# Sign bits of decoded weights on GpSimd, squares on ScalarE, and more operands inside the plan

## The chip, the cores and the metric

One core of one Trainium2 chip runs the whole kernel. The metric is the device time of one execution in microseconds (us). TensorE (PE) has its weight loads beside it (PEld); VectorE is DVE, ScalarE is ACT, GpSimd is POOL, and SyncE (SP) issues most transfers. Line numbers "L450" are those of the kernel before; after the change a line's number is higher, by one up to L449, by seven from L459 on (L601 becomes L608), by up to nine near the end.

## The reference

```python
def _attn_ref(q, k, v, sampled_blocks):          # q, k, v: (4, 8, 768, 64)
    scores = scale * np.matmul(q, k.transpose(0, 1, 3, 2))
    ...   # block 32: neighbours, first and last block, and 3 sampled blocks per block row are kept
    attn = np.exp(scores - max); attn = attn / (sum(attn) + 1e-09)
    return np.matmul(attn, v)
def _moe_ref(x, w_in, w_out, s, b):              # x (3072, 512), w_in (512, 2048), w_out (2048, 512)
    h = x @ w_in
    r = np.maximum(h, 0.0)
    g = s * (r * r) + b
    return (g @ w_out)
```

The attention's output, laid out again as 3072 tokens of 512 numbers, is x. The weights w_in and w_out come as 64-bit floats.

## The kernel before

**Three stages.** From 0 to some 246 us the kernel does the block-sparse attention. From there to 378.6 us it does the first 32 blocks of the MLP, "the planned MLP stage". A block i is 128 hidden rows f by 384 tokens g. It has twelve matmuls mlp1(i) (384 columns) into the bank h; then relu (L443, ACT), square, hidden_high (L454: times s and plus b on ACT; L455: rounded to the high part gh on ACT), hidden_low (L459: the rest, the low part, on DVE); and nine matmuls mlp2(i) (512 columns, L480 to L482) that need gh and the low part, one block later. From 378.6 us to the end the rest of the tokens is done in products of half blocks, written out by hand: for each of eight passes p and each s from 1 to 3 seven products n in the order 1, 2, 6, 7, 5, 3, 4 (a Strassen-like scheme). Twelve matmuls of L617 make two products. Their operands are sums S1 to S4 of quarters of the weights and T1 to T4 of quarters of x, and the quarters A11 to A22, B11 to B22. An operand is split into a high part (cast on ACT, L599) and a low part (subtraction on DVE, L601). The first product of a pass is copied out of its bank by ACT (L1456); n = 2, 5, 3 and 4 are "taken" by DVE (L627 and L628, or L1465 for a sum ahead of it), and the output blocks (L480 to L482) stand between products.

**Names of operand steps.** "<T1" loads a quarter, "+S1" or "+T1" adds (L575, L577, L580), "wA21" puts a quarter of the weights together from its two parts (L584), "hS1" is the high part, "lS1" the low part, ">A21" writes a quarter back. Which steps are done in the planned stage and which at a product is written out in tables: `early` items in the plan, EARLY (behind the last two blocks, 30 and 31, which are written out), FIRST (at the products of the first pass), and F_NEXT (later passes).

**Weights.** Each of 32 tiles of 128 × 512 weights (16 of w_in, 16 of w_out) is decoded by `decode_f64` from its 64-bit words: two masks on DVE (L85, L87), a copy of 16-bit halves on GpSimd (L88), a sign on ACT (L89: Sign of the upper word in place, after both masks), two activations on ACT (L91, L92) that make the magnitude, the product of magnitude and sign on DVE (L93, the high part), its exponent (L94), and the low part (L95). Three raw tiles are used in turn. Six weights are decoded during attention, 26 beside the planned MLP blocks.

**The order of the work.** A list scheduler (`Plan`) orders the first two stages, up to block 29: every operation has a given engine, a cost in ns and a priority, and each engine's program is written in the order in which the scheduler would start them. Engines take their programs in order, so one that waits holds up what is behind it. Attention's softmax works in groups: four masked maxima (L966), the copy of a transposed tile (L1017), a reciprocal (L989, L990), and the scaled block xss (L1064), which TensorE transposes (L1070).

Of the kernel before, what the change touches and what calls it, by code (L numbers as in the profile page):

```python
# [9 lines left out]
F32 = mybir.dt.float32  # L10
# [3 lines left out]
U16 = mybir.dt.uint16  # L14
AF = mybir.ActivationFunctionType
ALU = mybir.AluOpType
# [23 lines left out]
def decode_f64(nc, n, src, top, most, raw_of, mag_of, low_of, hi_of, lo_of):  # L40
# [32 lines left out]
    def hi():  # L73
        return get("hi", hi_of)
# [4 lines left out]
    def low_half(k):  # L79
        return low(U16).rearrange("p (n two) -> p n two", two=2)[:, :, k]  # L80

    A, V, G = nc.scalar, nc.vector, nc.gpsimd
# [6 lines left out]
        ("a", lambda: A.activation(word(1).bitcast(F32), word(1).bitcast(F32), AF.Sign), (0, 1)),  # L89
# [3 lines left out]
        ("v", lambda: V.tensor_tensor(out=hi(), in0=mag(F32), in1=word(1).bitcast(F32), op=ALU.mult), (3, 5)),  # L93
# [119 lines left out]
def kernel(  # L213
# [238 lines left out]
    def hidden_high(i):  # L452
        t, gh = htile(i % 2), htile(2 + i % 3)
        nc.scalar.activation(t, t, AF.Identity, bias=sb_b, scale=sb_s if i >= T["SQ"] else 1.0)  # L454
        nc.scalar.copy(gh, t)  # L455

    def hidden_low(i, eng=None):
        t, gh = htile(i % 2), htile(2 + i % 3)
        (eng or nc.vector).tensor_tensor(out=htile(5 + i % 3), in0=t, in1=gh.bitcast(F32), op=ALU.subtract)  # L459
# [201 lines left out]
    with ExitStack() as es:  # L661
# [665 lines left out]
        cost = (400, 420, 800, 670, 720, 720, 550, 390, 690)  # L1327
# [13 lines left out]
        for k, (which, f) in enumerate((w[0], int(w[1:])) for w in T["WL"].split()):  # L1341
# [5 lines left out]
            for m in range(pieces):  # L1347
                last_load = op("s", 450, wat - 4 + 4 * m, lambda load=load, m=m, n=pieces: load(m, n), [prev_k], alloc=[] if m else [raw], use=[raw] if m else [],
                                order=[last_load, *[y for x, y in pv_at if x <= wat - 4 + 4 * m][-1:]] if k < EARLY_W else [last_load, xl[(0, 1)]], nbytes=524e3 / pieces, late=T["LATE"])
                loads.append(last_load)  # L1350
# [29 lines left out]
        for k in range(NPL):  # L1380
            g, f = subs[k]
            for c in range(NCC):
                pm = op("p", 490, N + T["M1"] + k, lambda k=k, c=c: mlp1(k, (c,)), cols=1152, deps=[*ends, xs_ops[(g, c, 1)], wdone[("i", f, 8)], hd.get((k - 2, 0))], order=[pm])
            dep = pm
            for m, (eng, c, fn) in enumerate((("a", 480, relu), ("a" if k >= T["SQ"] else "v", 510, square), ("a", 960, hidden_high), ("g" if k < T["LOW"] else "v", 1100 if k < T["LOW"] else 420, hidden_low if k >= T["LOW"] else lambda i: hidden_low(i, nc.gpsimd)))):
                dep = hd[(k, m)] = op(eng, c, N - 50 + k, lambda k=k, fn=fn: fn(k), [dep, o_t, hd.get((k - 2, 3)) if m == 0 else None,
                                      m2.get(k - 3) if m == 2 else None])
            if k > 0:
                g, f = subs[k - 1]
                pm2 = m2[k - 1] = op("p", 1930, N + T["M2"] + k, lambda k=k: mlp2(k - 1), cols=4608, deps=[*every, hd[(k - 1, 3)], wdone[("o", f, 8)]], order=[pm2])  # L1390
# [4 lines left out]
        def early(deps, what):  # L1395
            rest = what[1:] not in ("B11", "B21")
            eng = {"h": "a", "<": "s", ">": "s"}.get(what[0], "v")
            wide = what[1] in "BT"
            cost = {"a": 980 if wide else 350, "s": 450, "v": 950 if wide else 420}[eng]

            def fn():
                ready_first()
                if rest:
                    ready_rest()
                work(0, S0, what)

            ew[what] = op(eng, cost, N + 600 + len(ew), fn, [*(over if rest else [m2[14], m2[15], last_load]), *(ew[x] for x in deps.split())],
                          nbytes={"<": 393e3, ">": 131e3}.get(what[0], 0))
# [19 lines left out]
    FIRST = {2: "lT1 lS1 wA12 +S4 hS4 hB22", 6: "lS4 +T4 hT4", 7: "lB22", 5: "lT4"}  # L1428
# [5 lines left out]
    EARLY = {30: "hT3 lT3 hS3 lS3", 31: "<B22 hT2 lT2 hT1 hS1"}  # L1434
# [128 lines left out]
```

## Time and profile before

| | |
|---|---|
| median of three runs (770.6, 777.41, 770.78) | 770.78 us |
| profiled execution | 773.25 us, of which the span is 771.5 |
| busy | PE 730.2, PEld 618.8, DVE 561.4, ACT 473.2, POOL 241.1 us |
| attention, to about | 246 us |
| planned MLP stage, to about | 378.6 us |

The span lies 1.75 us inside the profiled execution's time. The windows below give an engine's busy time in a stretch; a row of the timeline names in brackets how long the engine sat idle ahead of it, and for whom. Several instructions of the same kind in a row are one line, with their count.

### The profile page before, as it was taken

The page shows a single profiled execution, that of the slowest core. Times are in us where ns is not written, and L with a number is a line of the kernel's source. Part 1 is how long each engine was busy: PE and PEld are TensorE (multiplying, and loading weights), DVE is VectorE, ACT ScalarE, POOL GpSimd, SP SyncE. Part 2 cuts the span into 40 slices and gives each one's busy share as a digit, 9 for nine tenths or more (in the row PEclk, how much of TensorE's full clock was granted, in tenths as well). Part 3 has the DMA queues.
Part 4 walks back from the last instruction along what each step waited for, and adds up shares of the span by engine and source line. Part 5 has one row for each costly group of instructions (what it writes and reads, how often), then busy time and mean ns, then how long its engine had stood idle before and what let it go on. Part 6 is the DMA issues. An engine that isn't in the chain of part 4 may idle for free.

```text
span 771.5 us, 21375 instructions
## 1 busy us (share of the span) xinstructions
PE 730.2 (95%) x8032; PEld 618.8 (80%) x8032; DVE 561.4 (73%) x1433; ACT 473.2 (61%) x1141; POOL 241.1 (31%) x398
## 2 busy tenths in 40 slices
PE   8799798799888999999989999999999999999997
PEld 6376675477566989999878998888998998888896
DVE  4667576688786789887896678687678679666652
ACT  3657576688776877789753444565444467444443
POOL 4846255345430121222022232223222232222221
PEclk9989999999999999999999999999999999999999
DMA  9987988857873534635433222224000022000002
GB/s 243 221 214 206 249 218 234 215 159 211 226 199 106 151 110 147 209 119 161 99 125 91 76 84 74 62 69 123 1 1 1 1 62 82 1 1 0 1 1 82
DMA packets 101110, 89.41 MB, mean 116 GB/s; under 512 B 50192, under 2 KB 79504, under 8 KB 101008
## 3 DMA queue, kind: packets, MB, share of 16 engines
q1 hardware_dynamic: 98704, 81.76, 37.7%
q0 software_dynamic: 2304, 6.29, 3.3%
q8 instruction: 63, 1.03, 0.6%
q14 instruction: 39, 0.32, 0.1%
HBM read 69.15 MB, written 14.68 MB: 109 GB/s over the span
## 4 chain that ended last, share of the span: by engine, by line
PE 76%; DVE 7%; ACT 5%; DMA 5%; issue 4%; POOL 1%; SPq 1%; POOLq 0%; ACTq 0%; DVEq 0%
PE m L617 20%; PE o L481 10%; PE o L482 10%; PE o L480 10%; PE s L949 5%; PE xs L1058 5%; PE t L1006 5%; PE h L438 2%; PE h L440 2%; PE h L439 2%; PE od L1048 2%; DMA xd<-xst 2%; PE xs L1070 1%; DMA qr_3s<-in_q_dup_dram 1%; DVE ptile L966 1%
## 5 line engine op out<-in xcount | busy, mean ns | idle before, releaser
L459 POOL TENSOR_TENSOR hid<-hid,hid 128x384 fp32r<-128x384 f32 x96 | 105.3, 1098 | 292.9 <-ACT hid L635 249.4
L634 ACT ACTIVATE hid<-hid,sb_b,sb_s 128x384 f32<-128x384 f32 x96 | 68.1, 710 | 152.2 <-DVE hid L628 152.2
L978 ACT ACTIVATE ptile<-ptile,nm 128x256 f32<-128x256 f32 (+1 forms) x208 | 107.3, 519 | 35.7 <-DVE nm L966 35.3
L966 DVE CUSTOM_DVE_ANT_1 ptile<-s,mt 128x256 f32<-128x256 f32 x176 | 64.4, 421 | 31.9 <-PE s L949 29.6
L482 PE MATMUL o<-woutr,hid 128*128 128x512 f32 x168 | 66.4, 395 | 0.0
L481 PE MATMUL o<-woutr,hid 128*128 128x512 f32 x168 | 66.3, 395 | 0.0
L480 PE MATMUL o<-woutr,hid 128*128 128x512 f32 x168 | 65.3, 389 | 0.0
L617 PE MATMUL m<-wout,win 128*128 128x384 f32 x264 | 62.6, 340 | 2.1 <-ACT xrest L1456 1.6
L1058 PEld LDWEIGHTS xs<-vA,pt 128*32 128x32 f32 x1696 | 36.0, 113 | 29.0 <-ACT xst L1075 8.2
L617 PE MATMUL m<-xp,wop 128*128 128x384 f32 x288 | 58.3, 337 | 0.0
L1006 PE MATMUL t<-ident,ptile 128*128 128x128 f32 x352 | 51.4, 289 | 6.7 <-ACT ptile L978 3.8
L628 DVE SCALAR_TENSOR_TENSOR hid<-hid 128x384 f32<-128x384 f32 x96 | 54.7, 569 | 3.3
L1058 PE MATMUL xs<-vA,pt 128*32 128x64 f32 x1696 | 48.0, 227 | 9.5 <-issue 4.3
L481 PE MATMUL o<-win,hid 128*128 128x512 f32 x144 | 56.8, 395 | 0.0
L617 PE MATMUL m<-xp,win 128*128 128x384 f32 x288 | 55.1, 338 | 1.4 <-DVE xp L601 0.7
L617 PEld LDWEIGHTS m<-xp,win 128*128 128x128 f32 x288 | 50.9, 188 | 4.6 <-DVE xp L601 1.2
L635 ACT CAST hid<-hid 128x384 fp32r<-128x384 f32 x96 | 49.4, 515 | 7.8 <-ACT hid L634 0.7
L617 PEld LDWEIGHTS m<-xp,wop 128*128 128x128 f32 x288 | 51.5, 188 | 2.1
L617 PEld LDWEIGHTS m<-wout,win 128*128 128x128 f32 x264 | 47.4, 188 | 5.1 <-ACT xrest L1456 2.5
L1006 PEld LDWEIGHTS t<-ident,ptile 128*128 128x128 f32 x352 | 39.1, 145 | 14.4 <-ACT ptile L978 5.7
L888 POOL COPY kk<-kt 128x256 f32<-128x256 f32 (+2 forms) x46 | 20.9, 457 | 93.8 <-PE s L949 93.7
L482 PE MATMUL o<-win,hid 128*128 128x512 f32 x126 | 49.8, 395 | 0.0
(187 smaller groups left out, 1859.0 us busy)
## 6 DMA issues: line engine op xcount, KB each, us to landing
vB<-in_v_dram SPq DMA_DIRECT2D x109, 128.0 KB, 3.7
vA<-in_v_dram SPq DMA_DIRECT2D x72, 128.0 KB, 3.9
raw_o<-in_w_out_dram SPq DMA_DIRECT2D x14, 512.0 KB, 3.3
raw_i<-in_w_in_dram SPq DMA_DIRECT2D x12, 512.0 KB, 3.8
xd<-xst SPq DMA_DIRECT2D x44, 128.0 KB, 3.5
out_dram<-ob SPq DMA_DIRECT2D x20, 256.0 KB, 2.0
sum<-xd SPq DMA_DIRECT2D x12, 384.0 KB, 4.2
kt<-in_k_blk_dram SPq DMA_DIRECT2D x8, 384.0 KB, 5.4
```

What stands on the lines that cost most here:

```text
L459: (eng or nc.vector).tensor_tensor(out=htile(5 + i % 3), in0=t, in1=gh.bitcast(F32), op=ALU.subtract)
L480: nc.tensor.matmul(acc, gh[:, tsl], wout(f, 0), start=first, stop=False)
L481: nc.tensor.matmul(acc, gh[:, tsl], wout(f, 1), start=False, stop=False)
L482: nc.tensor.matmul(acc, gl[:, tsl], wout(f, 0), start=False, stop=last)
L617: nc.tensor.matmul(to, w_, x_, start=(c == 0 and k == 0), stop=(c == 1 and k == 2))
L628: vec.scalar_tensor_tensor(out=t, in0=t, scalar=0.0, in1=t, op0=ALU.max, op1=ALU.mult)
L634: nc.scalar.activation(t, t, AF.Identity, bias=sb_b, scale=sb_s)
L635: nc.scalar.copy(gh, t)
L966: nc.vector.tensor_tensor_reduce(out=pt, in0=sp, in1=msk, scale=-scale, scalar=FMAX if g == 0 else nm[:, 0:1], op0=ALU.add, op1=ALU.min, a ...
L978: nc.scalar.activation(pt[:, :w], pt[:, :w], AF.Exp, bias=nms[n][:, last:last + 1], scale=-1.0, accum_out=dns[i][:, g, j:j + 1])
L1006: nc.tensor.transpose(tp[:, (2 * j + c) * P:(2 * j + c + 1) * P], src[:, c * P:(c + 1) * P], ident)
L1058: nc.tensor.matmul(xs[quads[pair]], pt[:, c, quads[pair]], vt[:, a, col:col + D], start=(j == 0 and c == 0), stop=(c == 1), tile_position= ...
```

## The change

(a) The sign leaves ACT: GpSimd compares the upper 16 bits with 2^15 and multiplies by −2, which leaves 0 or −2 as a 16-bit number in the raw tile; this step waits for the load alone. L93 becomes (sign + 1) × magnitude in one DVE instruction (SCALAR_TENSOR_TENSOR). (b) The squares of blocks 10 to 23 go from DVE (L450) to ACT (L448). (c) For blocks 0 to 9, whose square holds the factor s already, hidden_high is one activation into the high part instead of two steps, and hidden_low adds b and subtracts on DVE in one instruction. (d) The plan's costs are new, and the extra delay that it gives to raw loads goes from 3000 to 700 ns for the weights beside the MLP. (e) T4, hT2, lT2, hS3, lS3, hS1, lS1, S4, hS4, lS4 and others are steps of the plan and no longer of FIRST and EARLY; B11 and B21 wait for mlp2(18) and not for the last raw load.

```diff
-        ("a", lambda: A.activation(word(1).bitcast(F32), word(1).bitcast(F32), AF.Sign), (0, 1)),
+        ("g", lambda: G.tensor_scalar(out=half(0).bitcast(I16), in0=half(3), scalar1=2.0 ** 15, scalar2=-2.0, op0=ALU.is_ge, op1=ALU.mult), ()),
...
-        ("v", lambda: V.tensor_tensor(out=hi(), in0=mag(F32), in1=word(1).bitcast(F32), op=ALU.mult), (3, 5)),
+        ("v", lambda: V.scalar_tensor_tensor(out=hi(), in0=half(0).bitcast(I16), scalar=1.0, in1=mag(F32), op0=ALU.add, op1=ALU.mult), (3, 5)),
...
-    "WARM": 4, "FILL": 4, "FP": -1.0, "NPL": 30, "SQ": 24, "LATE": 3000.0, "M1": 75.6, "M2": 77.7,
+    "WARM": 4, "FILL": 4, "FP": -1.0, "NPL": 30, "SQ": 10, "LATE": 3000.0, "M1": 75.6, "M2": 77.7,
...
     def hidden_high(i):
-        nc.scalar.activation(t, t, AF.Identity, bias=sb_b, scale=sb_s if i >= T["SQ"] else 1.0)
-        nc.scalar.copy(gh, t)
+        if i < T["SQ"]:
+            nc.scalar.activation(gh, t, AF.Identity, bias=sb_b)
+        else:
+            nc.scalar.activation(t, t, AF.Identity, bias=sb_b, scale=sb_s)
+            nc.scalar.copy(gh, t)
...
     def hidden_low(i, eng=None):
+        if i < T["SQ"]:
+            nc.vector.scalar_tensor_tensor(out=htile(5 + i % 3), in0=t, scalar=sb_b, in1=gh.bitcast(F32), op0=ALU.add, op1=ALU.subtract)
+            return
...
-        cost = (400, 420, 800, 670, 720, 720, 550, 390, 690)
+        cost = (420, 460, 900, 900, 720, 720, 690, 460, 740)
...
-                                order=[...], nbytes=524e3 / pieces, late=T["LATE"])
+                                order=[...], nbytes=524e3 / pieces, late=T["LATE"] if k < EARLY_W else 700.0)
...
-        for deps, what in (("", "<B11"), ("", "<B21"), ("", "<T1"), ("", "<T3"), ("", "<T2"), ("", "<T4"), ("<B11", "hB11"), ("hB11", "lB11"),
-                           ("<B21", "hB21"), ("hB21", "lB21"), ("", "wA21"), ("", "wA22"), ("wA21 wA22", "+S1"), ("", "wA11"), ("+S1 wA11", "+S2"),
-                           ("+S2", "hS2"), ("<T3 <T1", "+T3"), ("+T3 <T2", "+T1"), ("+T1", "+T2"), ("hS2", "lS2"),
-                           ("+S2", "+S3"), ("+S3", ">A21")):
+        for deps, what in (("", "<B11"), ("", "<B21"), ("<B11", "hB11"), ("hB11", "lB11"), ("<B21", "hB21"), ("hB21", "lB21"),
+                           ("", "<T1"), ("", "<T3"), ("", "<T2"), ("", "<T4"), ("", "wA21"), ("", "wA22"), ("wA21 wA22", "+S1"), ("", "wA11"),
+                           ("+S1 wA11", "+S2"), ("+S2", "hS2"), ("hS2", "lS2"), ("+S2", "+S3"), ("+S3", ">A21"), ("<T3 <T1", "+T3"),
+                           ("+T3 <T2", "+T1"), ("+T1", "+T2"), ("+T2", "hT2"), ("hT2", "lT2"), ("+S3", "hS3"), ("hS3", "lS3"), ("+S1", "hS1"),
+                           ("hS1", "lS1"), ("", "wA12"), ("wA12 +S2", "+S4"), ("+S4", "hS4"), ("hS4", "lS4"), ("+T2 <T4", "+T4")):
...
-    FIRST = {2: "lT1 lS1 wA12 +S4 hS4 hB22", 6: "lS4 +T4 hT4", 7: "lB22", 5: "lT4"}
+    FIRST = {2: "hB22", 6: "hT4", 7: "lB22", 5: "lT4"}
...
-    EARLY = {30: "hT3 lT3 hS3 lS3", 31: "<B22 hT2 lT2 hT1 hS1"}
+    EARLY = {30: "hT3 lT3 hT1", 31: "<B22 lT1"}
```

TensorE's program is in the same order before and after; those of ACT, DVE, POOL and SP are not. Three places follow.

ACT at the end of the planned stage, before. L599 with 128x256 is the high part of a sum of weights (hS2 goes into "win", hS3 into "wop"), with 128x12x2x32 that of a quarter of x or a sum T; L443, L448, L454, L455 are blocks 30 and 31.

```order
L599 CAST wout_5727<-wout_5727 128x12x2x32 x2
L599 CAST win_6239<-sum_6565 128x256
L443 ACTIVATE hid_5456<-h_15_6587 128x384
L448 ACTIVATE hid_5456<-hid_5456 128x384
L454 ACTIVATE hid_5456<-hid_5456,sb_b,sb_s 128x384
L455 CAST hid_5474<-hid_5456 128x384
L599 CAST xp_6605<-sum_6564 128x12x2x32
L599 CAST wop<-sum_6564 128x256
L443 ACTIVATE hid_5481<-h_15_6610 128x384
```

The same place after the change, from block 30 to the copy of the first product (L1456 before, L1465 now).

```order
L444 ACTIVATE hid_5456<-h_15_6588 128x384
L449 ACTIVATE hid_5456<-hid_5456 128x384
L458 ACTIVATE hid_5456<-hid_5456,sb_b,sb_s 128x384
L459 CAST hid_5471<-hid_5456 128x384
L606 CAST xp_6606<-sum_6452 128x12x2x32
L606 CAST xp_6606<-sum_6451 128x12x2x32
L444 ACTIVATE hid_5480<-h_15_6610 128x384
L449 ACTIVATE hid_5480<-hid_5480 128x384
L458 ACTIVATE hid_5480<-hid_5480,sb_b,sb_s 128x384
L459 CAST hid_5494<-hid_5480 128x384
L1465 COPY xrest<-m_6640 128x384
```

Ahead of block 30 no cast of a sum of weights is left; between blocks 30 and 31 stand two casts of sums of x (hT3, hT1), and the copy follows block 31 directly.

DVE at the same time, before: from the low part of block 29 (L459) on.

```order
L459 TENSOR_TENSOR hid_5534<-hid_5481,hid_5515 128x384
L93 TENSOR_TENSOR win_6239<-wkhp_427,raw_o_6455 128x512
L94 TENSOR_SCALAR wkhp_427<-win_6239 128x512
L95 SCALAR_TENSOR_TENSOR win_6239<-wklp_543,wkhp_427 128x512
L601 TENSOR_TENSOR wout_5727<-wout_5727 128x768 x2
L584 TENSOR_TENSOR whole<-win_5761 128x256 x2
L575 TENSOR_TENSOR sum_6563<-whole 128x256
L584 TENSOR_TENSOR whole<-win_2922 128x256
L575 TENSOR_TENSOR sum_6565<-sum_6563,whole 128x256
```

After: the rows from the low part of block 26 (now L466, first row) through that of block 27 (eighth row) to that of block 28 (last row).

```order
L466 TENSOR_TENSOR hid_5544<-hid_5456,hid_5537 128x384
L608 TENSOR_TENSOR win_6141<-sum_6453,win_6141 128x256
L608 TENSOR_TENSOR wop<-sum_6452,wop 128x256
L587 TENSOR_TENSOR sum_6452<-sum_6452,sum_6451 128x768
L582 TENSOR_TENSOR sum_6454<-sum_6455,sum_6453 128x256
L587 TENSOR_TENSOR sum_6451<-sum_6451,sum_6453 128x768
L587 TENSOR_TENSOR sum_6453<-sum_6453,sum_6452 128x768
L466 TENSOR_TENSOR hid_5482<-hid_5480,hid_5471 128x384
L608 TENSOR_TENSOR win_6141<-sum_6454,win_6141 128x256
L584 TENSOR_TENSOR sum_6454<-sum_6453,sum_6454 128x768
L608 TENSOR_TENSOR win_6141<-sum_6453,wout_5689 128x12x2x32
L466 TENSOR_TENSOR hid_5504<-hid_5456,hid_5494 128x384
```

The sums and low parts of the operands, which came behind the low part of block 29 and the last decode, now stand ahead of the low part of block 28, and all decodes ahead of that of block 25.

DVE in the attention's last third, before: the end of a softmax group (the row L966 is its last masked maximum) and its scaled block xss43.

```order
L966 ISA ptile7_86,nm167_4633<-s165_4569,mt_118 128x256
L966 ISA nm167_4633 128x1
L94 TENSOR_SCALAR wkhp0_426<-win0_2922 128x512
L1017 COPY pt160_0_4651<-t160_0_4637 128x512
L95 SCALAR_TENSOR_TENSOR win0_2922<-wklp0_542,wkhp0_426 128x512
L989 TENSOR_SCALAR rc43_4659<-dn43_4426 128x4
L990 RECIPROCAL rc43_4659<-rc43_4659 128x4
L1064 TENSOR_TENSOR xss43_4663<-xs43_4594,rc43_4659 128x256
```

After, from the same maximum on (now L973; the mask of the exponent is L95 now, the low part L96), and on to the next group's block xss44.

```order
L973 ISA ptile7_86,nm167_4644<-s165_4572,mt_118 128x256
L973 ISA nm167_4644 128x1
L1071 TENSOR_TENSOR xss43_4648<-xs43_4598,rc43_4467 128x256
L1024 COPY pt160_0_4656<-t160_0_4639 128x512
L95 TENSOR_SCALAR wkhp0_426<-win0_2922 128x512
...
L96 SCALAR_TENSOR_TENSOR win0_2922<-wklp0_542,wkhp0_426 128x512
L1024 COPY pt164_0_4750<-t164_0_4734 128x512
L996 TENSOR_SCALAR rc44_4756<-dn44_4524 128x4
L997 RECIPROCAL rc44_4756<-rc44_4756 128x4
L1071 TENSOR_TENSOR xss44_4760<-xs44_4689,rc44_4756 128x256
```

The block xss43 comes ahead of the copy and the decode steps that it stood behind. The next one, xss44, which stood directly behind its maxima, now stands behind a decode's low part, a copy and its reciprocal.

More of the change, by code (lines that the diff above doesn't have):

```diff
@@ L14 @@
 U16 = mybir.dt.uint16
+I16 = mybir.dt.int16
 AF = mybir.ActivationFunctionType
@@ L1348 @@
                 last_load = op("s", 450, wat - 4 + 4 * m, lambda load=load, m=m, n=pieces: load(m, n), [prev_k], alloc=[] if m else [raw], use=[raw] if m else [],
-                                order=[last_load, *[y for x, y in pv_at if x <= wat - 4 + 4 * m][-1:]] if k < EARLY_W else [last_load, xl[(0, 1)]], nbytes=524e3 / pieces, late=T["LATE"])
+                                order=[last_load, *[y for x, y in pv_at if x <= wat - 4 + 4 * m][-1:]] if k < EARLY_W else [last_load, xl[(0, 1)]], nbytes=524e3 / pieces, late=T["LATE"] if k < EARLY_W else 700.0)
                 loads.append(last_load)
@@ L1389 @@
                 g, f = subs[k - 1]
-                pm2 = m2[k - 1] = op("p", 1930, N + T["M2"] + k, lambda k=k: mlp2(k - 1), cols=4608, deps=[*every, hd[(k - 1, 3)], wdone[("o", f, 8)]], order=[pm2])
+                pm2 = m2[k - 1] = op("p", 2090, N + T["M2"] + k, lambda k=k: mlp2(k - 1), cols=4608, deps=[*every, hd[(k - 1, 3)], wdone[("o", f, 8)]], order=[pm2])
         ew = {}
```

7 lines of the change are left out of this document (4 added, 3 removed), and 2 rows, old and new, of the table T.

## The prediction

> **What bounds the kernel now.** I read the busy shares and the chain of waits on the page, then the busy time by stretches, then TensorE's timeline where a stretch isn't full.
>
> ```profile
> PE   730.2 (95%) x8032; PEld 618.8 (80%) x8032; DVE 561.4 (73%) x1433; ACT 473.2 (61%) x1141; POOL 241.1 (31%) x398
> PE 76%; DVE 7%; ACT 5%; DMA 5%; issue 4%; POOL 1%; SPq 1%; POOLq 0%; ACTq 0%; DVEq 0%
> 260.00:360.00 100.00, 100.00 (x503) 90.57 (x502) 86.31 (x160) 82.40 (x147) 20.07 (x22) 1.00 0.44 138
> 380.00:400.00 20.00, 17.68 (x81) 14.51 (x82) 18.53 (x33) 14.56 (x28) 4.68 (x4) 1.00 0.31 112
> ```
>
> A stretch's columns are its length, then busy time of PE, PEld, DVE, ACT and POOL, then the clock. TensorE makes three quarters of the chain and is full for the whole planned MLP stage, with DVE at 86 of 100 us: relieving ACT or DVE there shortens nothing by itself. It isn't full at 380 to 400, the junction from planned blocks to written-out products; there the change can pay. TensorE across the junction, then in a later, regular pass:
>
> ```profile
> 378.58 1.22 PE L617 MATMUL m<-wout,win 128*128 128x384 f32 x6
> 380.30 1.32 PE L617 MATMUL m<-wout,win 128*128 128x384 f32 x6 [0.49 <-ACT hid L443]
> 384.29 0.44 PE L617 MATMUL m<-wout,win 128*128 128x384 f32 x1 [0.58 <-ACT xrest L1456]
> 390.57 1.15 PE L617 MATMUL m<-xp,win 128*128 128x384 f32 x5 [0.36 <-DVE xp L601]
> 392.43 0.41 PE L617 MATMUL m<-xp,win 128*128 128x384 f32 x1 [0.71 <-DVE sum L1465]
> 393.20 1.15 PE L617 MATMUL m<-xp,win 128*128 128x384 f32 x5 [0.36 <-DVE xp L601]
> 401.87 0.44 PE L617 MATMUL m<-wout,win 128*128 128x384 f32 x1 [1.02 <-ACT xrest L1456]
> ...
> 409.31 2.26 PE L617 MATMUL m<-xp,win 128*128 128x384 f32 x12
> 411.41 0.39 PE L480 MATMUL o<-win,hid 128*128 128x512 f32 x1
> 413.49 2.27 PE L617 MATMUL m<-wout,win 128*128 128x384 f32 x12
> ```
>
> In the regular pass two products take 411.41 − 409.31 = 2.10 us and an output block 2.08. From 378.58 to 401.87, 23.29 us, stand nine products and four output blocks, worth 9 × 1.05 + 4 × 2.08 = 17.8. So **5.5 us are lost at the junction**, and no more can be won there.
>
> **The junction's term.** ACT works in order, and is held up by one cast:
>
> ```profile
> 376.17 0.41 ACT L599 CAST win<-sum 128x256 fp32r<-128x256 f32 x1 [4.21 <-DVE sum L575]
> 376.48 0.48 ACT L443 ACTIVATE hid<-h 128x384 f32<-128x384 f32 x1
> 378.72 0.83 ACT L599 CAST xp<-sum 128x768 fp32r<-128x768 f32 x1
> 379.76 0.48 ACT L443 ACTIVATE hid<-h 128x384 f32<-128x384 f32 x1
> 383.77 0.47 ACT L1456 COPY xrest<-m 128x384 f32<-128x384 f32 x1
> ```
>
> hS2 waited 4.21 us for S2 from DVE, and relu(30), relu(31) and the copy of the first product (L1456) stood behind it. In the order after, hS2, hS3 and hT2 come ahead of block 30, hS1 too, only hT3 and hT1 (0.83 each) remain between relu(30) and relu(31), and the copy follows block 31 at once. With relu(30) started some 2 us earlier, relu(31) ends near 379 instead of 380.24, and the copy can run near 381. That takes away the delay at 380.30 (0.67 against 378.58 + 1.05) and at 384.29 (0.84: its wait, and the slower matmuls behind it). On DVE the tail loses four subtractions and a sum of 256 columns and two operations of 768, near 4 us, so lB22 comes in time (0.8 at 390.57). At 392.43 and 393.20 three products stand back to back, and L1465 and lT4 still come behind the step that takes the fifth product: of 1.7 us I leave 1.4. At 401.87 (1.4 with the products ahead of it) DVE has less debt, but the copy still stands behind hS4 of the next pass; I take 0.9. Sum: 0.67 + 0.84 + 0.8 + 0.3 + 0.9 = **−3.5 us**; the bounds are 0 (each wait is replaced by its neighbour) and −5.5.
>
> **The planned MLP stage.** DVE gets more to do ahead of block 28's low part (365.04), which mlp2(28) (370.27) needs.
>
> ```profile
> 365.04 0.56 DVE L459 TENSOR_TENSOR hid<-hid,hid 128x384 fp32r<-128x384 f32 x1 [0.23 <-ACT hid L455]
> 372.39 1.82 DVE L601 TENSOR_TENSOR wout<-wout 128x768 fp32r<-128x768 f32 x2
> 374.12 0.76 DVE L584 TENSOR_TENSOR whole<-win 128x256 f32<-128x256 f32 x2
> 374.91 0.43 DVE L575 TENSOR_TENSOR sum<-whole 128x256 f32<-128x256 f32 x1
> 376.95 2.94 DVE L580 TENSOR_TENSOR sum<-sum,sum 128x768 f32<-128x768 f32 x3
> 370.27 0.39 PE L480 MATMUL o<-woutr,hid 128*128 128x512 f32 x1
> L450 DVE SCALAR_TENSOR_TENSOR hid<-hid,sb_s 128x384 f32<-128x384 f32 x24 | 15.4, 640 | 4.2 <-ACT hid L443 4.0
> L94 DVE TENSOR_SCALAR wkhp<-win x17: 407/427/893, 149.7 to 371.2; 128x512 int32<-128x512 int32 x17
> L95 DVE SCALAR_TENSOR_TENSOR win<-wklp,wkhp x17: 682/693/1175, 150.5 to 371.8; 128x512 fp32r<-128x512 int32 x17
> L94 DVE TENSOR_SCALAR wkhp<-win 128x512 int32<-128x512 int32 x11 | 6.1, 553 | 0.3
> L95 DVE SCALAR_TENSOR_TENSOR win<-wklp,wkhp 128x512 fp32r<-128x512 int32 x11 | 9.4, 854 | 1.1
> L88 POOL COPY wklp<-raw_i x16: 753/780/1236, 127.8 to 354.3; 128x512 uint16<-128x512 uint16 x16
> L459 POOL TENSOR_TENSOR hid<-hid,hid 128x384 fp32r<-128x384 f32 x96 | 105.3, 1098 | 292.9 <-ACT hid L635 249.4
> L89 ACT ACTIVATE raw_i<-raw_i x16: 664/680/715, 128.8 to 361.1; 128x512 f32<-128x512 f32 x16
> ```
>
> The squares that leave: 14 × 0.64 = −9.0. The decode steps that in the old order stood behind this row and now ahead: the two masks of one weight (near 0.9) and twice L93 to L95 (0.69 + 0.43 + 0.69), 4.6. lB11 and lB21: 1.8. The chain of S and T, which before began at 374.12: four additions L584 and four L575, four small low parts, three sums L580 (2.94), T4 and lT2 (0.95 each), 9.8. Net +7.2. L93 in its new form costs what L95, the same operation, costs: 0.69, as before.
>
> To that comes disturbance by GpSimd, the change's own risk. The rows show it from the copy L88 alone: between 250 and 380 us L94 on the w_in halves takes 0.553 on average against a median of 0.427, L95 0.854 against 0.693. That is 0.29 us per weight for a copy of 0.78. The sign on GpSimd isn't in this trace: it reads and writes 16-bit numbers of the same count as L88, the nearest row; the other end is L459, 32 bits with two inputs, 1.098 × 512/384 = 1.46. I take 0.85, so 0.3 us more per weight and 26 × 0.3 = 7.8. Together +15.0. The cover: 100 − 86.31 = 13.7 us of idle DVE before 360, and the low part's lead, 370.27 − 365.60 = 4.7: 18.4 us. So the planned stage still costs **0**, with 3 us to spare, and what isn't covered TensorE would wait out one to one. ACT goes the easy way: −26 × 0.68 for the signs, +14 × 0.53 for squares, −10 casts of 0.51, some 15 us less than its 82.
>
> The Trainium skill speaks against this move: "SBUF — State Buffer", section "Who interferes with whom", says that a vector operation with two inputs in SBUF contends with a GpSimd instruction that reads SBUF, and that the loser blocks for the whole instruction. By that rule each sign would cost DVE its own length; the maxima above (L95 1.175, L94 0.893) agree that DVE is held, though by 0.5 us and not by the copy's 0.78, and in most cases not at all. It is the first rival below that would come true by this page.
>
> **Attention's end.** The plan has new costs, and so DVE does decode steps at other places among the softmax groups. TensorE needs a group's scaled block (xss, L1064) for its transposes (L1070).
>
> ```profile
> L1064 DVE TENSOR_TENSOR xss<-xs,rc x18: 419/422/426, 162.1 to 236.4; 128x256 f32<-128x256 f32 x18
>   PE xs L1070: 3.5, 4
> 213.41 0.42 DVE L94 TENSOR_SCALAR wkhp<-win 128x512 int32<-128x512 int32 x1
> 213.74 0.68 DVE L1017 COPY pt<-t 128x512 f32<-128x512 f32 x1
> 215.83 0.44 PE L1070 MATMUL xs<-ident,xss 128*128 128x128 f32 x2 [1.79 <-DVE xss L1064]
> 215.80:219.20 3.40, 3.37 (x99) 2.41 (x99) 1.93 (x12) 1.67 (x6) 1.71 (x5) 0.69 0.46 148
> 219.20:222.60 3.40, 3.40 (x84) 2.69 (x84) 2.26 (x7) 2.23 (x7) 0.74 (x2) 0.81 0.52 156
> ```
>
> Four times TensorE waited for it, 3.5 us in all. In the order after, the group of 215.83 has nothing in front: −1.8, and −1.7 for the clock that fell behind it ((0.31 + 0.19) × 3.4). The three others lose 1.2 more, as a copy of 0.68 moves behind one of them. But three groups that had nothing or little ahead now have a decode step and a copy or two there, 1.3 to 1.7 us each, 4.4 in all; part of it is slack, so I take half, 2.2, and one new fall of the clock, 1.7. Sum −1.8 − 1.7 − 1.2 + 2.2 + 1.7 = **−1 us**, with bounds −4.7 (no new wait) and +4.8 (every new wait in full, and three falls of the clock).
>
> **Sum.** −3.5 + 0 − 1 = −4.5 us on the profiled execution's 773.25 (span 771.5 and 1.75 around it): 768.75. That execution stands 0.3% above the median, 770.78; in the same ratio the median becomes **766.3 us**, −0.6%. A measurement of this kernel tells about 1% from no change (its runs lie between 770.6 and 777.41).
>
> **Rivals.**
> - *DVE becomes the bound of the planned stage (slower side).* Price: if GpSimd blocks DVE for a whole sign each time, 26 × 0.85 = 22, DVE gets 7.2 + 22 = 29 more against 18.4 of cover, 11 us of waits at mlp2 of the late blocks, less the 4.5: 770.78 + 6.3 = 777. It decides from 0.6 us per sign on ((18.4 + 4.5 − 7.2)/26); half unusable idle lowers that to 0.34. For it: DVE at 86 of 100, and the plan's lighter raw loads pull decode steps forward, ahead of low parts. Against it: the traced blocking of 0.3 per copy. Chance 0.2, spread over 770 to 782.
> - *Attention's end goes well, or badly.* Well: with −4.7 and a junction of −4, 762; 0.15. Badly: +4.8 − 3.5, 772; 0.1.
> - *The junction is not helped:* the copy L1456, lT4 or a raw operand is late in its turn, term 0 to −1. Result 769.5; 0.15. For it: 380 to 400 has DVE at 18.53 of 20, and only 4 us leave it.
> - *The change doesn't do what it says:* L93 waits for a late sign as it did for ACT, up to 0.85 on a weight. GpSimd is busy for 20 of 100 us there and a sign waits for the load alone, so I see it only as a small part of the first rival, within its chance.
>
> **How the numbers follow.** Forecast 0.4, rivals 0.2, 0.25 and 0.15. The likeliest is 766.3. The range takes in 762 and less (both gains full, 770.78 − 5.5 − 4.7 = 760.6) and the first rival up to 775; a tenth lies beyond each end. Faster by over 1% (below 763.1) 0.2, within 1% 0.7, slower by over 1% (above 778.5) 0.1.
>
> **What would show it.** After: the waits at 380.30 and 384.29 of that place gone, the junction near 19.8 instead of 23.29 us; the sign between 0.75 and 1.0 us on GpSimd; L94 and L95 of the decode no more than 0.3 us longer per weight; TensorE 100.00 of 100 in the planned stage; no wait of 1.8 us at L1070 near 215. Wrong is the prediction if TensorE waits for low parts of blocks 20 to 29, or if the sign takes over 1.3 us.

## The result: slower by 2.9%

| | before | after |
|---|---|---|
| median | 773.68 us (770.6 to 777.41, 4 runs) | 799.54 us (791.06 to 800.34, 4 runs) |
| ratio, with its 95% interval | | 1.0289 (1.024 to 1.0339) |
| span of the profiled execution | 771.5 us | 798.6 us |

I had forecast 766.3 us, with 0.1 for slower by over 1%. The page of the changed kernel, the stretch that was full before, one row of GpSimd, and what TensorE and ACT waited for:

```profile
PE 741.5 (93%) x8032; PEld 624.3 (78%) x8032; DVE 590.9 (74%) x1419; ACT 459.3 (58%) x1113; POOL 334.8 (42%) x430
PE 58%; DVE 13%; ACT 5%; issue 4%; DMA 2%; SPq 0%; DVEq 0%; ACTq 0%
260.00:360.00 100.00, 90.75 (x438) 80.70 (x437) 97.09 (x132) 60.84 (x107) 81.76 (x42) 0.97 0.45 139
L90 POOL TENSOR_SCALAR raw_i<-raw_i x16: 2689/2886/3177, 132.1 to 369.1; 128x512 int16<-128x512 uint16 x16
PE h L439 <- ACT hid L444: 12.9, 8, 2.2
ACT wkhp L92 <- DVE wkhp L86: 29.8, 21, 4.0
```

ACT's row for the same step in the kernel before (mask L85, activation L91), whose last two numbers are the idle time ahead of it:

```profile
L91 ACT ACTIVATE wkhp<-wkhp,b_top 128x512 f32<-128x512 int32 x26 | 18.7, 719 | 2.7 <-DVE wkhp L85 2.6
```

TensorE falls from 76 to 58% of the chain and DVE rises from 7 to 13%. In the planned stage DVE is now at 97 of 100 us and TensorE at 91. The sign takes 2.89 us (minimum, median and maximum stand in that order), where I had put 0.85 with 1.46 as the upper end. A row of waits gives us in total, how often, and the longest. TensorE waits 12.9 us for the relu on ACT, which frees the bank of mlp1 (the place that TensorE writes its sums to); before, it waited for no relu in this stage. ACT isn't busy (61 of 100 us): it stands 29.8 us in the planned stage for the first mask of the decode on DVE, against 2.6 before. One case, at 318 us:

```profile
318.08 0.72 ACT L92 ACTIVATE wkhp<-wkhp,b_top 128x512 f32<-128x512 int32 x1 [3.09 <-DVE wkhp L86]
318.71 0.69 ACT L458 ACTIVATE hid<-hid,sb_b,sb_s 128x384 f32<-128x384 f32 x1
319.43 0.51 ACT L459 CAST hid<-hid 128x384 fp32r<-128x384 f32 x1
319.85 0.72 ACT L93 ACTIVATE wkhp<-wkhp,b_most 128x512 int32<-128x512 f32 x1
320.48 0.47 ACT L444 ACTIVATE hid<-h 128x384 f32<-128x384 f32 x1
321.00 0.44 PE L439 MATMUL h<-xp,win 128*128 128x384 f32 x1 [1.98 <-ACT hid L444]
```

ACT stood 3.09 us for a mask on DVE (L86); the relu is four steps behind it in ACT's order, and TensorE stood 1.98 us for the relu. In the planned stage TensorE's waits add up to 15.0 us (0.6 before), of which one of 1.0 is for a low part. Its matmuls, the same as before, are busy 137.3 us instead of 131.5, at a granted clock of 0.98 instead of 1.00.

Where the 27.1 us of the span are, from the start of mlp1(0), of the first product and of product n = 6 of the second pass:

| stage | before | after | difference |
|---|---|---|---|
| attention, to mlp1(0) | 246.5 | 255.5 | +9.0 |
| planned MLP stage | 132.1 | 152.3 | +20.2 |
| junction | 23.3 | 20.8 | −2.4 |
| rest | 369.6 | 369.9 | +0.3 |

### The profile page after: what moved, and what is told of

Same layout as the page of the kernel before. It is cut to its first block, busy times and chain, and to the rows that moved or that the text cites. A ratio compares the mean times of both kernels' runs of the same rounds, so it can differ in the third digit from the quotient of the medians.

```text
span 798.6 us, 21348 instructions
## 1 busy us (share of the span) xinstructions
PE 741.5 (93%) x8032; PEld 624.3 (78%) x8032; DVE 590.9 (74%) x1419; ACT 459.3 (58%) x1113; POOL 334.8 (42%) x430
## 4 chain that ended last, share of the span: by engine, by line
PE 58%; DVE 13%; ACT 5%; issue 4%; DMA 2%; SPq 0%; DVEq 0%; ACTq 0%
PE m L624 20%; PE o L488 9%; PE o L489 9%; PE o L487 9%; PE xs L1065 3%; PE s L956 2%; PE t L1013 2%; DVE wkhp L86 2%; DVE wklp L88 1%; PE h L439 1%; PE h L441 1%; PE h L440 1%; DVE wkhp L95 1%; PE od L1055 1%; ACT wkhp L93 1%
## 5 line engine op out<-in xcount | busy, mean ns | idle before, releaser
L466 POOL TENSOR_TENSOR hid<-hid,hid 128x384 fp32r<-128x384 f32 x96 | 104.8, 1092 | 302.8 <-ACT hid L642 280.0
L973 DVE CUSTOM_DVE_ANT_1 ptile<-s,mt 128x256 f32<-128x256 f32 x176 | 64.5, 420 | 39.6 <-PE s L956 36.9
L488 PE MATMUL o<-win,hid 128*128 128x512 f32 x144 | 56.8, 394 | 0.0
L439 PE MATMUL h<-xp,win 128*128 128x384 f32 x112 | 39.8, 355 | 13.1 <-ACT hid L444 12.9
L90 POOL TENSOR_SCALAR raw_i<-raw_i 128x512 int16<-128x512 uint16 x16 | 46.3, 2894 | 10.1 <-DVE wout L96 4.4
```

What stands on the lines that cost most here:

```text
L488: nc.tensor.matmul(acc, gh[:, tsl], wout(f, 1), start=False, stop=False)
L973: nc.vector.tensor_tensor_reduce(out=pt, in0=sp, in1=msk, scale=-scale, scalar=FMAX if g == 0 else nm[:, 0:1], op0=ALU.add, op1=ALU.min, a ...
```

## The experiments

"Stages" below are attention / planned stage / junction of the profiled execution, in us. Theory A is that the sign on GpSimd is the loss, B that the order and the other parts lose as well.

**sign_on_act.** The changed kernel without part (a).

```diff
-        ("g", lambda: G.tensor_scalar(out=half(0).bitcast(I16), in0=half(3), ...), ()),
+        ("a", lambda: A.activation(word(1).bitcast(F32), word(1).bitcast(F32), AF.Sign), (0, 1)),
...
-        cost = (420, 460, 900, 900, ...)
+        cost = (420, 460, 900, 670, ...)
```

> The changed kernel with the sign back on ACT (activation Sign, and the product of magnitude and sign as a plain TENSOR_TENSOR), all else as changed. Theory A, the sign on GpSimd is the whole loss: the planned stage returns from 152 to about 132 us, attention ends near 247 instead of 255 us, and what is left is the junction's gain of 2.4 us, so 768 to 771 us, ratio about 0.996. Theory B, the new costs and the new order of the plan lose too: attention still ends at 252 us or later, or the planned stage still takes over 136 us, 776 to 785 us.

780.95 us, ratio 1.0088 (1.0055 to 1.0121); stages 245.3 / 135.5 / 25.7. Most of the loss is gone, so A holds for its larger part. But it is still slower than before, in the planned stage (+3.4, just under B's 136) and at the junction (+2.4), which I had expected to gain: the total lies in B's band.

**before_sign_pool.** The kernel before with part (a) alone.

```diff
-        ("a", lambda: A.activation(word(1).bitcast(F32), word(1).bitcast(F32), AF.Sign), (0, 1)),
+        ("g", lambda: G.tensor_scalar(out=half(0).bitcast(I16), in0=half(3), ...), ()),
...
-        ("v", lambda: V.tensor_tensor(out=hi(), in0=mag(F32), in1=word(1).bitcast(F32), op=ALU.mult), (3, 5)),
+        ("v", lambda: V.scalar_tensor_tensor(out=hi(), in0=half(0).bitcast(I16), scalar=1.0, in1=mag(F32), op0=ALU.add, op1=ALU.mult), (3, 5)),
```

> The kernel before with the sign on GpSimd alone; the plan still has its old costs and order rules. Theory A: the sign takes 2.9 us, POOL gets 93 us and DVE's decode steps beside it grow by 0.2 to 0.5 us each, so the planned stage takes 150 us or more and the whole 790 to 805 us, ratio 1.025 to 1.04. Theory B, the loss comes from the order or the other parts: below 780 us.

788.44 us, ratio 1.0194 (1.0145 to 1.0242); stages 246.0 / 149.4 / 21.4. The sign alone costs 17.3 us of the planned stage, where all parts together cost 20.2. Stage and total lie just under A's bands. The junction is shorter by 1.9 us with no operand step moved: TensorE comes late, relu(30) on ACT waits for TensorE (1.99 us) and no longer behind a cast that waits for a sum, and TensorE's waits ahead of the second product and for the copy of the first are gone.

**plan_knows.** The changed kernel with the plan told the sign's length.

```diff
-        cost = (420, 460, 900, 900, ...)
+        cost = (420, 460, 900, 2900, ...)
```

> The changed kernel with the plan told 2900 ns instead of 900 for the sign. Theory A1, the resource is short (DVE held while GpSimd works, whatever the order): still 793 us or more, ratio above 1.02. Theory A2, the order is what hurts, since the plan thinks the sign done 2 us before it is and puts DVE steps in front that wait: the planned stage falls to 140 us or less and the whole to below 787 us.

788.89 us, ratio 1.0196 (1.0149 to 1.0243); stages 249.2 / 145.1 / 20.9. Both bands were missed, it lies between them: a truer cost gives back 7 us of the planned stage, and 13 stay lost in this order.

**sign_by_itself.** The kernel before and behind its end a row of instructions on tiles of their own.

```diff
...
+    for fn in (pool_copy, pool_sign, pool_sign_one, pool_sign_flat, pool_f32_two, pool_f32_mult, pool_f32_sub):
+        for _ in range(3):
+            fn()
...
+    masks(4)
+    subs(4)
+    both(masks, 20, pool_sign, 4)
+    both(subs, 20, pool_sign, 4)
+    both(masks, 12, pool_copy, 6)
+    both(subs, 12, pool_copy, 6)
```

> The kernel before with a tail behind its end, whose time is not of interest: GpSimd alone runs the copy of 16-bit halves, the sign, the sign with one operation, the sign on adjacent numbers, and 32-bit forms, three times each; then DVE runs masks (one input) and subtractions (two inputs) alone, then beside the sign and beside the copy. Theory A, the sign is slow by itself: 2.7 to 2.9 us with nothing beside it. Rival C, it is slow because DVE holds GpSimd up: below 1.3 us alone, and near 2.9 only beside DVE. For DVE: if it is held by any GpSimd instruction that reads, masks and subtractions beside the sign take 0.4 us more at times, and beside the copy as well; if the sign's long reading is what holds, only beside the sign.

`both(masks, 20, pool_sign, 4)` lets DVE run 20 masks (the form of L85) while GpSimd runs 4 signs. First GpSimd's forms three times each, then DVE's two groups beside signs and two beside copies, from the timeline (start, length, count at the end); the last three rows give minimum, median and maximum in ns of the sign, the mask and the subtraction:

```profile
770.59 2.46 POOL L1503 COPY mb<-mb 128x512 uint16<-128x512 uint16 x3 [7.45 <-DVE mb L1497]
773.00 8.57 POOL L1506 TENSOR_SCALAR mb<-mb 128x512 int16<-128x512 uint16 x3
781.65 6.80 POOL L1509 TENSOR_SCALAR mb<-mb 128x512 int16<-128x512 uint16 x3
788.54 5.93 POOL L1512 TENSOR_SCALAR mb<-mb 128x512 int16<-128x512 uint16 x3
794.56 5.93 POOL L1515 TENSOR_SCALAR mb<-mb 128x512 f32<-128x512 f32 x3
805.30 3.94 POOL L1521 TENSOR_TENSOR mb<-mb,mb 128x512 f32<-128x512 f32 x3
...
809.79 14.85 DVE L1529 TENSOR_SCALAR mb<-mb 128x512 int32<-128x512 int32 x20
825.17 13.13 DVE L1533 TENSOR_TENSOR mb<-mb 128x384 f32<-128x384 f32 x20
838.85 8.09 DVE L1529 TENSOR_SCALAR mb<-mb 128x512 int32<-128x512 int32 x12
847.47 9.36 DVE L1533 TENSOR_TENSOR mb<-mb 128x384 f32<-128x384 f32 x12
...
L1506 POOL TENSOR_SCALAR mb<-mb x11: 2647/2659/2910, 773.0 to 833.1; 128x512 int16<-128x512 uint16 x11
L1529 DVE TENSOR_SCALAR mb<-mb x36: 418/430/1532, 771.6 to 846.5; 128x512 int32<-128x512 int32 x36
L1533 DVE TENSOR_TENSOR mb<-mb x36: 557/559/943, 774.6 to 856.3; 128x384 f32<-128x384 f32 x36
```

DVE was still at work until 777.24 us, on a memset and on the first four masks and subtractions, so the three copies and the first two signs (2.85 and 2.91 us) are not alone. The third sign is, and takes 2.65 us, so rival C falls: it is long by itself. From there on GpSimd is alone: one operation instead of two takes 2.21 (781.65), adjacent numbers 1.92 (788.54), 32-bit numbers with the same two operations 1.92 as well. The copy of as many 16-bit numbers takes 0.76 to 0.83.

For DVE, a mask alone starts every 0.46 us (0.43 long). Twenty of them took 14.85 us beside four signs, instead of 9.2: **1.4 us lost per sign**, which the single masks show as one of 1.53 and one of 0.73 to 0.77 for each sign. Twenty subtractions of 0.56 (one each 0.59) took 13.13 instead of 11.8: 0.33 per sign. Beside a copy a mask takes 0.86 instead of 0.43 and a subtraction 0.94 instead of 0.56: 0.4 per copy. So DVE is held by both instructions, not by the sign alone, while the sign beside DVE's masks takes 2.66 to 2.71 us, hardly longer than alone.

**sign_unread.** The kernel before, ACT's sign in use, and GpSimd's sign written as well, into halves that nobody reads.

```diff
+        ("g", lambda: G.tensor_scalar(out=half(0).bitcast(I16), in0=half(3), ...), ()),
...
-        cost = (400, 420, 800, 670, 720, 720, 550, 390, 690)
+        cost = (400, 420, 800, 670, 720, 720, 550, 390, 690, 900)
```

> The kernel before, with the sign on ACT as it was, and GpSimd's sign written as well, into halves of the raw tile that nobody reads. Theory H, DVE is held while GpSimd works: the planned stage still takes 145 us or more (132 before, 149 in before_sign_pool) and the whole 785 us or more. Theory W, it was the wait for a late sign: nothing waits for it here but the raw tile's next load, so the planned stage takes 136 us or less and the whole at most 780 us.

784.4 us, ratio 1.0132 (1.0083 to 1.0181); stages 244.8 / 143.4 / 23.1, and DVE is as full as in the changed kernel:

```profile
260.00:360.00 100.00, 96.79 (x474) 86.42 (x473) 96.61 (x147) 74.18 (x133) 82.27 (x43) 0.98 0.40 127
```

The times lie a little under H's bands and well above W's. With no product waiting for GpSimd's sign, 11.3 of the sign's 17.3 us remain. The decode steps on DVE, the same as before, take some 20 us longer in the planned stage, so I take the 11.3 for DVE's holding by GpSimd. The raw tile is also released later, but DVE never waits for a raw load in this stage's trace; ACT's sign waits twice for GpSimd's, 2.4 us together. What makes the other 6, the wait of the product of magnitude and sign or the order, isn't taken apart.

**operands_only.** The kernel before with part (e) alone.

```diff
-            ew[what] = op(eng, cost, N + 600 + len(ew), fn, [*(over if rest else [m2[14], m2[15], last_load]), ...
+            ew[what] = op(eng, cost, N + 600 + len(ew), fn, [*(over if rest else [m2[14], m2[15], m2[18]]), ...
...
-                           ("+S2", "hS2"), ("<T3 <T1", "+T3"), ("+T3 <T2", "+T1"), ("+T1", "+T2"), ("hS2", "lS2"), ...
+                           ("+S1 wA11", "+S2"), ("+S2", "hS2"), ..., ("hS3", "lS3"), ("+S1", "hS1"), ..., ("+T2 <T4", "+T4")):
...
-    FIRST = {2: "lT1 lS1 wA12 +S4 hS4 hB22", 6: "lS4 +T4 hT4", 7: "lB22", 5: "lT4"}
+    FIRST = {2: "hB22", 6: "hT4", 7: "lB22", 5: "lT4"}
...
-    EARLY = {30: "hT3 lT3 hS3 lS3", 31: "<B22 hT2 lT2 hT1 hS1"}
+    EARLY = {30: "hT3 lT3 hT1", 31: "<B22 lT1"}
```

> The kernel before with part (e) alone: the longer list of operand steps in the plan, the shorter FIRST and EARLY. In ACT's order five casts of sums (hS3, hS2, hS1, hS4, hT2) stand ahead of relu(30). Theory J1, casts that wait for DVE's sums hold relu(30) up: TensorE waits 2 to 3 us ahead of the first product and about as long ahead of the second, the junction takes 25 us or more (23.3 before), and the whole loses 3 to 6 us. Theory J2, as I predicted: the junction takes 20 us or less and the whole gains 2 to 4 us.

780.12 us, ratio 1.0066 (1.0041 to 1.0091); stages 246.7 / 137.1 / 25.1. The junction follows theory J1, as ACT's and TensorE's rows show:

```profile
376.51 0.41 ACT L599 CAST wop<-sum 128x256 fp32r<-128x256 f32 x1 [3.23 <-DVE sum L575]
377.30 0.41 ACT L599 CAST win<-sum 128x256 fp32r<-128x256 f32 x1 [0.39 <-DVE sum L575]
379.44 0.41 ACT L599 CAST win<-sum 128x256 fp32r<-128x256 f32 x1 [1.40 <-DVE sum L575]
382.51 0.84 ACT L599 CAST wout<-sum 128x768 fp32r<-128x768 f32 x1 [2.66 <-DVE sum L580]
383.25 0.48 ACT L443 ACTIVATE hid<-h 128x384 f32<-128x384 f32 x1
...
387.48 2.29 PE L617 MATMUL m<-wout,win 128*128 128x384 f32 x6 [2.38 <-ACT hid L443]
```

Where one cast waited for DVE ahead of relu(30) before, four do now, 7.7 us together, and relu(30) starts at 383.25 instead of 376.48. The steps that I counted as taken away from the junction had been put in front of it. Ahead of the first product, though, TensorE waits only 0.3 us for the relu. More of the planned stage's 5.0 us is another wait, which neither theory named: at 372 and 373 us TensorE stands 1.8 and 0.8 us for the last decoded tile of w_out (L93, L95 on DVE). In sign_on_act the waits are as J1 has them, 3.0 us ahead of the first product and 2.4 ahead of the second, both for the relu.

**no_sign_no_operands.** Parts (b), (c) and (d) alone: sign_on_act with the old operand lists.

```diff
...
-    FIRST = {2: "hB22", 6: "hT4", 7: "lB22", 5: "lT4"}
+    FIRST = {2: "lT1 lS1 wA12 +S4 hS4 hB22", 6: "lS4 +T4 hT4", 7: "lB22", 5: "lT4"}
...
-    EARLY = {30: "hT3 lT3 hT1", 31: "<B22 lT1"}
+    EARLY = {30: "hT3 lT3 hS3 lS3", 31: "<B22 hT2 lT2 hT1 hS1"}
```

> The changed kernel with the sign back on ACT and the old operand lists, so parts (b), (c) and (d) alone: squares of blocks 10 to 23 on ACT, one-step high parts, new costs. If the loss of sign_on_act (0.9%) came from the operand steps alone (J1), this is 768 to 775 us, no different from before. If the new costs and the new order lose as well: 778 us or more.

775.39 us, ratio 1.0024 (0.9992 to 1.0056); stages 244.5 / 132.4 / 23.1. No difference that can be measured: together the squares on ACT, the one-step high parts and the costs take 3.7 us off DVE in the planned stage (109.3 to 105.7) and put 3.4 on ACT (103.2 to 106.6), and TensorE, as full as before (131.5 us), gains nothing.

**hS2_behind.** The kernel before, hS2 and lS2 behind block 31.

```diff
-                           ("+S2", "hS2"), ("<T3 <T1", "+T3"), ("+T3 <T2", "+T1"), ("+T1", "+T2"), ("hS2", "lS2"),
+                           ("<T3 <T1", "+T3"), ("+T3 <T2", "+T1"), ("+T1", "+T2"), 
...
-    EARLY = {30: "hT3 lT3 hS3 lS3", 31: "<B22 hT2 lT2 hT1 hS1"}
+    EARLY = {30: "hT3 lT3", 31: "<B22 hS2 lS2 hT2 lT2 hS3 lS3 hT1 hS1"}
```

> The kernel before with hS2 and lS2 taken out of the plan and put behind block 31, so that no cast of a sum of weights stands ahead of relu(30). By J1 it is this cast's wait that delays the products of the junction: the waits ahead of the products 2 and 6 go, 1.5 us less at the junction, then 769 to 772.5 us against 774, unless hS2 comes late for the product n = 6 in its turn, which would leave the time where it was. By J2 no gain.

772.54 us, ratio 0.9982 (0.995 to 1.0014); stages 250.7 / 132.1 / 22.2. The wait at the second product is gone, that at n = 6 is 0.3 instead of 0.6, and the junction is 1.0 us shorter where J1 had 1.5; the time can't tell that from nothing. Its attention has the same program as before and ended 4.2 us later: so far single executions scatter.

**casts_behind.** hS2_behind, hS4 of the second pass behind the copy of its first product, and lT4 ahead of the taking of product 5.

```diff
...
-    F_NOW = {p: {1: "lS4"} for p in range(1, NFC // 2)}
+    F_NOW = {p: {1: "hS4 lS4" if p == 1 else "lS4"} for p in range(1, NFC // 2)}
-    FIRST = {..., 6: "lS4 +T4 hT4", 7: "lB22", 5: "lT4"}
+    FIRST = {..., 6: "lS4 +T4 hT4", 7: "lB22 lT4"}
...
-    F_NEXT[0] = {..., 4: "+S3 >A21 hS3 hS1 lS2 wA12 +S4 lS3 lS1 hS4"}
+    F_NEXT[0] = {..., 4: "+S3 >A21 hS3 hS1 lS2 wA12 +S4 lS3 lS1"}
```

> hS2_behind, and two steps more: hS4 of the second pass goes behind the copy of that pass's first product (it stood ahead of it, and TensorE waited 1.0 us at the second pass's n = 6), and lT4 goes ahead of the taking of product 5. J1: each step takes away its wait, 1.4 and 0.7 us of the junction beside the 1 us of hS2_behind, so 3 us in all against the kernel before: junction 20.5 to 21 us, ratio 0.996, 771 against 774 us. Rival J3, DVE is the bound at the junction and the wait turns up one product later: junction 22 us or more, ratio 0.998 to 1.

773.61 us, ratio 1.0001 (0.9972 to 1.0029); stages 245.3 / 132.3 / 23.2. The second pass's wait of 1.0 us is gone, but the bank of product 5 is freed later:

```profile
391.81 2.05 PE L617 MATMUL m<-xp,win 128*128 128x384 f32 x6 [2.15 <-DVE sum L1465]
```

lT4 stands now ahead of L1465 on a DVE that has no gap there; 0.71 us became 2.15. J3 holds for this step, and the junction is no shorter than before.

**bank_first.** casts_behind with lT4 where it was, and L1465 ahead of the taking steps.

```diff
-    FIRST = {..., 7: "lB22 lT4"}
+    FIRST = {..., 7: "lB22", 5: "lT4"}
...
-                    i = take((b, p + 8), to, part_sums["u2"], ALU.add)
                     vec.tensor_tensor(out=part_sums["u3"], in0=to, in1=part_sums["u1"], op=ALU.add)
+                    i = take((b, p + 8), to, part_sums["u2"], ALU.add)
```

> casts_behind without its step on lT4 (it stands behind the taking of product 5 again), and at product 5 the sum L1465, which frees the bank, goes ahead of the two taking steps instead of behind them. hS2 behind block 31 and hS4 of the second pass behind the copy stay. J1: without the wait of 2.1 us that lT4 made, TensorE waits for L1465 at most 0.3 us, and the junction takes 20.5 to 21.5 us against 23.3 before, 771 against 774 us, ratio 0.995 to 0.998. J3, DVE is the bound at the junction: over 22 us again, ratio 0.998 to 1.001.

773.13 against 774.35 us, ratio 0.998 (0.9956 to 1.0005); stages 246.3 / 131.9 / 20.7. The junction is 2.6 us shorter, inside J1's band and not J3's, and no wait for L1465 is left; of the first pass a wait of 0.96 us for lT4 is. TensorE's next wait comes in the second pass:

```profile
401.10 1.31 PE L617 MATMUL m<-xp,wop 128*128 128x384 f32 x6 [0.95 <-DVE hid L627]
```

The rest behind the junction takes 371.5 us instead of 369.6, so 1.9 of the 2.6 us are given back, about half of that at this wait, and the whole is not clear of zero. No version beats the kernel before beyond doubt.

**early_signs_on_act** and **changed_again**, on the attention's +9.0 us.

```diff
-        ("g", lambda: G.tensor_scalar(out=half(0).bitcast(I16), in0=half(3), ...), ()),
+        *([("a", lambda: A.activation(word(1).bitcast(F32), word(1).bitcast(F32), AF.Sign), (0, 1))] if act else [("g", ...)]),
...
-        return decode_f64(nc, NW, src, b_top, b_most, *tail, lambda: view(f, 0), lambda: view(f, 1))
+        return decode_f64(nc, NW, src, b_top, b_most, *tail, lambda: view(f, 0), lambda: view(f, 1), n < EARLY_W)
```

> The changed kernel with the signs of the six weights that are decoded during attention on ACT, as before; the 26 others stay on GpSimd. If the attention's longer time (255.5 against 246.5 us) comes from these six signs, attention ends at 248 us or earlier, the planned stage stays near 152 us and the whole falls to 790 to 793 us. If it is the scatter of an execution or the new order, attention may end anywhere from 244 to 256 us and the time stays at 797 to 800 us.

> The changed kernel once more, for a second look at its attention: with a cause in the program it ends at 253 to 257 us again; with scatter alone (the same attention program ended at 246.5 us in the kernel before and at 250.7 us in hS2_behind) it may end at 246 to 252 us. The planned stage takes 150 to 154 us, the junction 20 to 22 us.

With the six early signs on ACT: 794.19 us, ratio 1.0277 (1.0215 to 1.0339), stages 248.7 / 152.5 / 20.9. The attention (248) and the whole (790 to 793) lie a little above the bands for the early signs. The changed kernel again, one run: 797.38 us, stages 252.1 / 152.6 / 20.9, between its two bands for the attention.

The attention program of the kernel before ended at 246.5, 247.6, 246.7, 250.7, 245.3 and 246.3 us in six profiles (before, sign_by_itself, operands_only, hS2_behind, casts_behind and bank_first), the changed one's at 255.5 and 252.1. So the changed attention looks slower, by 1.4 us at the least and 6.6 on average, from two profiles. But plan_knows, whose ACT and DVE have the changed kernel's program up to there, ended at 249.2. And neither half of the change shows it by itself: with the signs on GpSimd and the plan's old costs (before_sign_pool) attention ended at 246.0, with the new costs and the signs on ACT (sign_on_act) at 245.3. The whole times of the changed kernel with and without the early signs don't differ by their intervals. The cause stays open.

## Why the prediction was wrong

**The bound of the planned stage: wrong by the price, and by the cover.** The step that failed is the term for GpSimd in DVE's sum: the price of the sign and of what it does to DVE. I priced 2.89 us at 0.85, from the 16-bit copy as the nearest row, and called 1.46 the other end, from a subtraction with two inputs. Neither row had the sign's two operations with a comparison, and the second was no upper end. And I took 0.3 us of disturbance per weight. The masks of the decode, by tile, after and then before:

```profile
L86 DVE TENSOR_SCALAR wkhp<-raw_o 128x512 int32<-128x512 int32 x14 | 11.3, 808 | 0.0
L86 DVE TENSOR_SCALAR wkhp<-raw_i 128x512 int32<-128x512 int32 x12 | 11.2, 937 | 0.0
L88 DVE TENSOR_SCALAR wklp<-raw_o 128x512 uint16<-128x512 uint16 x14 | 13.7, 977 | 0.0
L88 DVE TENSOR_SCALAR wklp<-raw_i 128x512 uint16<-128x512 uint16 x12 | 10.3, 858 | 0.0
...
L85 DVE TENSOR_SCALAR wkhp<-raw_o 128x512 int32<-128x512 int32 x14 | 5.9, 419 | 0.0
L85 DVE TENSOR_SCALAR wkhp<-raw_i 128x512 int32<-128x512 int32 x12 | 5.6, 469 | 0.0
L87 DVE TENSOR_SCALAR wklp<-raw_o 128x512 uint16<-128x512 uint16 x14 | 6.5, 461 | 0.0
L87 DVE TENSOR_SCALAR wklp<-raw_i 128x512 uint16<-128x512 uint16 x12 | 6.1, 509 | 0.0
```

The two masks took 46.5 us instead of 24.1 for 26 weights, 0.86 us more for each. All five DVE steps of the decode, summed the same way, took 108.0 instead of 77.5, so 1.17 us per weight and not 0.3. With that the sum of my own part on the planned stage is 7.2 + 26 × 1.17 = 37.6 against 18.4 of cover, 19 us over; 20.2 were measured.

That the two agree is an accident, for the cover was wrong too. DVE's busy time in the planned stage and the stage's length, by the windows of each profile, against the kernel before (109.3 of 132.1 us):

| | DVE busy, more by | stage, longer by | covered |
|---|---|---|---|
| before_sign_pool | 28.2 | 17.3 | 10.9 |
| sign_unread | 22.6 | 11.3 | 11.3 |
| plan_knows | 24.8 | 13.1 | 11.7 |
| changed kernel | 29.7 | 20.2 | 9.5 |

Of the 22.7 us in which DVE stood idle before, 9 to 12 took in more work, about half, and not the 18.4 that I counted. By my sum the sign alone, with no other work moved, would have cost under 10 us; it cost 17.3. "Half unusable idle", which I named beside the first rival, came nearer: 13.7 / 2 + 4.7 = 11.5. No run lies near the 0.6 or 0.34 us per sign from which I said the price decides, so that point isn't tested. The first rival came true in its mechanism, DVE as the bound, but not in its size: it ended at 782 us, and had 0.2.

**The path of the loss: partly right.** I had named mlp2 waiting for low parts of late blocks. TensorE waited for them 1.0 us. It waited mostly one step earlier, 12.9 us at mlp1 for a bank, through ACT: a decode activation that waits for a mask holds the relu behind it.

**The junction: the step failed, and its direction came mostly by another cause.** −3.5 was forecast, −2.4 came. But operands_only shows 1.8 us more, not 3.5 less: I read off that hS2, hS3, hT2 stood ahead of block 30 in ACT's order and took it that their sums would be ready by then. Of the five terms of the sum the first two (0.67 and 0.84, the waits ahead of the second product and for the copy of the first) are won in the changed kernel, but in before_sign_pool too, where no operand step moved: they are TensorE's lateness. The third (0.8, lB22) is won in the changed kernel and in operands_only, and not in before_sign_pool: it is the operand steps'. The last two (0.3 and 0.9) were not won: TensorE waits 0.75, 0.36 and 0.98 us at those places, as before. What I said of the mechanism, casts that hold the relu and the copy, is borne out for the relu by hS2_behind; for the copy and the bank, casts_behind and bank_first take the waits away, but not the time.

**ACT's relief, nothing: not contradicted, but not tested alone.** In the changed kernel ACT's busy time in the planned stage falls from 103.2 to 95.8 us and the stage grows. No run relieves ACT and nothing else; no_sign_no_operands, which moves work from DVE to ACT, gives 1.0024 with no change inside its interval.

**Attention: −1 forecast, +9.0 and +5.6 seen in two profiles.** Its upper bound of +4.8 was too low, and the waits that I counted there, of xss, did grow, from 3.5 to 5.5 us in both. One profile's waits of 0.3 to 1.8 us are no base for a term where executions of the same program scatter by 5 us.

The Trainium skill's rule in "SBUF — State Buffer", section "Who interferes with whom", spoke against the change, and the runs agree that the two engines contend. Its price, that the loser blocks for the whole instruction, is not what sign_by_itself shows: of a sign's 2.66 us beside DVE one mask loses 1.1 and another 0.3, a third runs its usual 0.43 us inside the sign, and a subtraction loses 0.36. The masks, with one input, lose more than the subtractions with two, of which the rule as I quoted it speaks.

## What to carry to other kernels

Before moving an operation to another engine, measure that very form of instruction alone and beside the receiving engine's neighbours: a copy of the same size said nothing of the sign's price. Where one engine is at 86% beside a full TensorE, count the slack of the stage and ask from which price per instruction it is used up, but don't count all of it: here about half of DVE's idle time could take in work. And an operand step that is put earlier in an in-order engine's program is only earlier if what it waits for is ready; else it holds up what stood behind it.

## What the runs showed of the hardware

- GpSimd's TENSOR_SCALAR with comparison and multiplication, 128 × 512 from 16-bit to 16-bit numbers at a stride of four: 2.65 us alone, 5.2 ns for each of 512; with the comparison alone 2.21, on adjacent numbers 1.92 (sign_by_itself). In the kernel its median is 2.89.
- DVE loses 1.4 us per such sign among masks with one input (0.43 us long, one of them 1.53), and 0.33 among subtractions with two; beside a GpSimd copy of 0.83 to 0.92 us each mask or subtraction loses 0.4 (sign_by_itself). Beside the signs of the changed kernel, each with a copy, the five DVE steps of a weight's decode lose 1.17 us together.
- The time of the same attention program scatters by 5 us between six executions (245.3 to 250.7), beside a spread of the whole kernel's runs of 12 us (768.37 to 780.45, on several chips; 768.37 to 777.99 on one).
